# One block of TensorE matmuls for the spread of 1/den, and fixed order lists, in a four-layer attention and FFN kernel

## The chip, the cores and the metric

The kernel runs on one core of a Trainium2 chip. The metric is the device time of one execution in microseconds (us), the median of several runs; lower is better. The engines of the core are named as in the profile: PE (TensorE, matmuls), PEld (its weight loads), DVE (VectorE), ACT (ScalarE), POOL (GpSimd) and SP (the queue that issues most DMAs).

## The reference, cut to what matters

```python
x = A_x                                   # 2048 tokens x 512, bfloat16
x = x + _A_ref(_layernorm(x), A_wqkv, A_wo)
x = x + _B_ref(_layernorm(x), B_w_gate, B_w_up, B_w_down)
x = x + _A_ref(_layernorm(x), A_wqkv, A_wo)
x = x + _B_ref(_layernorm(x), B_w_gate, B_w_up, B_w_down)

# A: linear attention, 32 heads of 16
phi = lambda t: jnp.where(t > 0, t + 1, jnp.exp(t)) + 1e-6
pq, pk = phi(q), phi(k)
kv  = einsum("bhsd,bhse->bhde", pk, v);   z = einsum("bhsd->bhd", pk)
num = einsum("bhqd,bhde->bhqe", pq, kv);  den = einsum("bhqd,bhd->bhq", pq, z) + 1e-6
A = (num / den) @ wo
# B: (silu(x @ w_gate) * (x @ w_up)) @ w_down, inner width 1792
```

Layers 0 and 2 are A, layers 1 and 3 are B.

## The kernel before, in words

The 2048 tokens are 16 tiles of 128 tokens, in four groups of 512. Everything stays in SBUF; each weight is read once. TensorE's program is the string `PROGRAM`, one token for one block of matmuls; the first digit is the layer:

- `S` is a warm-up matmul on zeros. `0t3` transposes tile 3 on PE; all other transposes are DMAs issued from SP.
- `0k3` projects the keys of tile 3, `0q21` the queries of group 2, chunk 1. Four matmuls of 512 columns each.
- `0g3` adds tile 3 into X'·phi(k), a sum that holds four PSUM banks over all sixteen tiles; `0z3` adds its keys into z (four matmuls of one column), in one bank more. `0v` and `0m0` to `0m3` turn that sum into the matrix that is applied to the queries.
- `0d21` is the part of den of group 2, chunk 1. After its fourth part DVE takes 1/den.
- `0w5` applies the matrix to the scaled queries of tile 5 and adds the result to x. It starts the layer norm of the next layer for that tile.
- `1u309` is gate and up of group 3, inner block 9 (eight matmuls); `1n5` is down of tile 5 (fourteen).

1/den stands by token and has to be spread over the queries, which stand transposed. For most groups ACT repeats it (L713) and a DMA transposes it (L717). For the groups named in `PE_T` (`0d2` and `2d1`) the function `rep_pe` does it on PE: the tokens `0r2a`, a = 0 to 3, multiply 32 rows of `rT` with 32 rows of the selector `esel`, into one PSUM bank, four matmuls of 128 columns for each a. DVE then multiplies the queries with that bank (L742, called pqn below). The four blocks stand apart in `PROGRAM`: `0r21 0r23 0w3 0r22 0w2 0w1 0r20 0w0`, and `2r10 2v 2q33 2m1 2m0 2m2 2m3 2w0 2d31 2r11 2d30 2w1 2r13 2w2 2w3 2r12`.

Every instruction is an `Op` with the buffers it reads and writes. The queues of ACT, DVE, POOL and SP are ordered by a planner, `Prog.schedule`: it plays PE's fixed order with a cost for each operation (`occ`, `lat`), a wait of `SEM` between engines, and takes at each step the ready operation with the earliest due time, shifted by a `BIAS` for its kind. `ON_ACT` says where work has a choice: `0x5` puts the last step of a layer norm (called apply below: L509 on ACT, L513 on DVE) on ACT, `0s4` the statistics of a tile in layer 0 (L486 and L489 on ACT, L478 and L480 on DVE), `0k5` or `0q21` one of the steps of phi (L561), `0G0` and `0M0` copies out of PSUM. `sync` turns the buffers into semaphore waits. Each engine runs its own queue strictly in order.

A layer norm is: statistics, vpe (L498, POOL or DVE), pow (L502, POOL, 1/sqrt), nmr (L506, POOL, only for an apply on ACT), apply, and the DMA transpose (L522, SP) into `xnT`. `bank()` gives the PSUM bank that was used longest ago and is not pinned. The weights Wo, Wg and Wu are nine DMAs on POOL that wait for all transposes of layer 0 (`after=a`); POOL has four DMA lanes, so its fifth DMA waits in POOL's queue until the first has landed. `mask` is built on POOL by a memset and two selects (L414, L415, L418); `0z` ends with a multiplication by it, called zm (L641, DVE), before the first `0d`.

Of the kernel before, what the change touches and what calls it, by code (L numbers as in the profile page):

```python
# [5 lines left out]
ACT = mybir.ActivationFunctionType  # L6
# [3 lines left out]
P = 128  # L10

SEM = 0.06
HOLD = 0.17
BIAS = {"aggr": -2.4, "apply": 2.89, "den": 5.86, "evac": 3.27, "exp": -1.25, "gst": 0.77, "h": 5.8, "id1":
        -1.31, "mask": 3.19, "negm": -2.54, "phi": -6.05, "pow": 9.11, "pqn": -5.7, "rT": 3.11, "rep":
        -15.2, "res": -0.19, "sq": 1.71, "stats": -6.49, "tanh": -7.7, "ts": 1.82, "vpe": -3.12, "xT": 2.81,
        "zm": 2.36}


class Op:  # L20
    __slots__ = ("i", "eng", "fn", "deps", "occ", "lat", "dma", "lane", "start", "end", "need", "val",
                 "dead", "succ", "pos", "prio", "kind")


class Prog:
# [5 lines left out]
    def __init__(self, lanes):  # L31
        self.ops = []
        self.bufs = {}
        self.lanes = lanes

    def op(self, eng, fn, r=(), w=(), occ=0.5, lat=None, after=(), dma=0.0, prio=None, kind=""):
        o = Op()
        o.i = len(self.ops)
        o.eng, o.fn, o.occ, o.dma, o.prio, o.kind = eng, fn, occ, dma, prio, kind
        o.lat = lat if lat is not None else occ + 0.09  # L40
        o.need = dma > 0
        o.succ = []
        deps = set(a.i for a in after if a is not None)
        for k in r:
            st = self.bufs.get(k)
            assert st is not None and st[0] is not None, f"read of {k} before a write"
            deps.add(st[0])
        for k in w:
            st = self.bufs.get(k)
            if st:  # L50
                if st[0] is not None:
                    deps.add(st[0])
                deps.update(st[1])
        for k in r:
            self.bufs[k][1].append(o.i)
        for k in w:
            self.bufs[k] = [o.i, []]
        deps.discard(o.i)
        o.deps = deps
        self.ops.append(o)  # L60
        return o

    def schedule(self):
        ops = self.ops
        for o in ops:
            for d in o.deps:
                ops[d].succ.append(o.i)
        t = sum(o.occ for o in ops if o.eng == "pe")
        after = t
        for o in reversed(ops):  # L70
            dead = t + 50.0
            for s in o.succ:
                s = ops[s]
                dead = min(dead, s.dead - o.lat - SEM)
            if o.eng == "pe":
                dead = after = min(dead, after - o.occ)
            o.dead = dead if o.prio is None else o.prio
        for o in ops:
            o.dead -= BIAS.get(o.kind, 0.0)
        nd = {o.i: len(o.deps) for o in ops}  # L80
        free = {e: 0.6 for e in self.ENGINES}
        free["act"] = 0.61
        avail = {e: [] for e in self.ENGINES}
        pe_q = [o for o in ops if o.eng == "pe"]
        pe_at = 0
        order = {e: [] for e in self.ENGINES}
        pipe = [0.0, 0.0]

        def ready_time(o):
            rt = 0.0  # L90
            for d in o.deps:
                p = ops[d]
                if p.eng == o.eng and o.eng == "pe":
                    continue
                rt = max(rt, p.end + SEM)
            return rt

        rt_of = {}

        def push(o):  # L100
            rt_of[o.i] = ready_time(o)
            if o.eng != "pe":
                avail[o.eng].append(o)

        for o in ops:
            if nd[o.i] == 0:
                push(o)
        left = len(ops)
        while left:
            best = None  # L110
            for e in self.ENGINES:
                if e == "pe":
                    if pe_at < len(pe_q) and nd[pe_q[pe_at].i] == 0:
                        o = pe_q[pe_at]
                        s = max(free[e], rt_of[o.i])
                        if best is None or s < best[0]:
                            best = (s, o)
                    continue
                if not avail[e]:
                    continue  # L120
                at = {o.i: max(free[e], rt_of[o.i]) for o in avail[e]}
                lim = min(at.values()) + HOLD
                o = min((o for o in avail[e] if at[o.i] <= lim), key=lambda o: (o.dead, o.i))
                if best is None or at[o.i] < best[0]:
                    best = (at[o.i], o)
            assert best is not None, "stuck"
            s, o = best
            o.start = s
            free[o.eng] = s + o.occ
            if o.dma:  # L130
                k = o.lat > 2.5
                pipe[k] = max(pipe[k], s + o.occ + 0.9) + o.dma
                o.end = pipe[k] + 0.6
            else:
                o.end = s + o.lat
            if o.eng == "pe":
                pe_at += 1
            else:
                avail[o.eng].remove(o)
            o.pos = len(order[o.eng])  # L140
            order[o.eng].append(o)
            left -= 1
            for k in o.succ:
                nd[k] -= 1
                if nd[k] == 0:
                    push(ops[k])
        self.order = order
        self.span = max(o.end for o in ops)
        return order

    def sync(self):
# [3 lines left out]
        for e in self.ENGINES:  # L155
            for o in order[e]:
                if o.dma:
                    n = self.lanes[e]
                    k = rr.get(e, 0)
                    rr[e] = (k + 1) % n  # L160
                    o.lane = f"q{e}{k}"
# [32 lines left out]
        for e in self.ENGINES:  # L194
            seen = {}
            for o in order[e]:
                ws = []
                for q, p in o.deps.items():
# [3 lines left out]
                    ws.append((p.end, q, p.val))  # L202
                ws.sort()
                self.waits[o.i] = [(q, v) for _, q, v in ws]
# [51 lines left out]
S S S S S S S S S 0t0 S S S S 0t3 0t1 0k0 0t2 0k1 0k2 0g0 0k3 0z0 0g1 0k4 0g2 0g3 0k5 0z4 0k10 0z2 0k9 0g4 0g5  # L256
0k6 0z10 0k7 0z9 0z3 0q03 0k8 0g10 0t15 0g7 0k15 0k13 0z5 0z8 0k12 0g9 0k11 0q11 0g6 0z15 0k14 0q10 0z13 0q02
0z7 0z1 0q01 0g11 0q00 0z14 0q12 0q21 0z12 0z6 0z11 0q13 0d02 0d03 0d01 0d00 0g8 0d11 0q20 0g13 0d12 0q22 0d13
0d10 0q23 0d20 0g15 0g12 0g14 0d23 0d22 0d21 0q30 0v 0q31 0m0 0m1 0m3 0m2 0r21 0r23 0w3 0r22 0w2 0w1 0r20 0w0
0q33 0w5 0w11 0w7 0w6 0w9 0q32 0d33 0w8 0w4 0w10 1u011 1u007 1u005 1u008 0d31 1u002 1u006 0d32 1u012 1u003  # L260
1u013 0d30 1u010 1u004 1u000 1u110 1u001 1u009 0w14 1n3 0w12 1n0 1u106 1n1 1u102 1n2 1u107 1u204 0w13 1u101
0w15 1u111 2k2 1u109 1u105 1u103 1u104 1u108 2k0 2k1 1u100 2q00 1u112 1u113 2k3 1n7 1n6 1u209 1u211 1u205 1n4
1n5 1u213 1u200 1u303 1u202 1u203 2q10 1u301 1u208 1u309 1u304 1u206 1u212 2g0 1u201 1u311 1u302 2q11 1u305
1u207 1u310 2q01 1u308 2q03 1u312 2q02 1u210 1n11 1u313 2k4 1u300 1n8 1n10 1u306 1n9 1u307 2k8 1n14 2k7 2k10
2k5 2q21 1n15 2k6 2k9 1n13 2k11 1n12 2q12 2k15 2k14 2g3 2g5 2q20 2q22 2z4 2k13 2q23 2z15 2z9 2z7 2g2 2k12 2z3
2z14 2g7 2z6 2z8 2z2 2z11 2g6 2z5 2z12 2z13 2z0 2g14 2z1 2z10 2q13 2d01 2g12 2g1 2d02 2d00 2d03 2d20 2d13 2d21
2d22 2q30 2d10 2d12 2g13 2g10 2d11 2d23 2q31 2g15 2g4 2g9 2g11 2g8 2q32 2r10 2v 2q33 2m1 2m0 2m2 2m3 2w0 2d31
2r11 2d30 2w1 2r13 2w2 2w3 2r12 2w6 2w5 2w11 2w4 2w8 2w7 2d32 2w9 2w10 2d33 3u008 3u000 3u009 3u013 3u010
3u004 3u003 3u005 3u007 3u103 3u110 3u108 3u012 3u002 3u001 3u006 3u104 2w13 3u011 3n3 2w12 3u100 3n2 3n0
3u106 3u105 3u107 3u111 3n1 2w14 3u102 3u109 3u112 3u101 3u113 3n4 3n5 3n6 3n7 3u200 3u201 3u202 3u203 3u204  # L270
2w15 3u205 3u206 3u207 3u208 3u209 3u210 3u211 3u212 3u213 3n8 3n9 3n10 3n11 3u300 3u301 3u302 3u303 3u304
3u305 3u306 3u307 3u308 3u309 3u310 3u311 3u312 3u313 3n12 3n13 3n14 3n15
"""

PE_T = set("""
0t0 0t1 0t2 0t3 0d2 0t15 2d1
# [5 lines left out]
0G0 0G2 0G3 0M0 0M2 0k11 0k13 0k14 0k15 0k3 0k4 0k5 0k6 0p0 0p14 0p15 0p2 0q00 0q01 0q03 0q11 0q12 0q22 0q30  # L282
0q31 0s4 0s8 0t0 0t12 0t13 0t14 0t2 0t3 0t4 0t5 0t6 0t7 0x1 0x10 0x11 0x12 0x15 0x5 0x6 0x7 0x8 1p11 1p5 1p6
1p8 1t0 1t10 1t13 1t14 1t3 1t8 1x1 1x10 1x11 1x12 1x14 1x2 1x4 1x5 1x6 1x8 1x9 2G0 2G2 2M0 2M2 2k0 2k1 2k10
# [627 lines left out]
```

## Time and profile before

| what | value |
|---|---|
| time, median of 4 runs | 432.83 us (432.17 to 433.08) |
| the profiled execution's own time | 432.01 us |
| its span | 430.3 us |
| PE busy | 420.9 us (98%), 2231 matmuls |
| DVE, ACT, POOL busy | 290.6, 215.0, 79.7 us |

The span is the profiled part of the execution; 1.7 us lie around it. "Busy" of PE counts pipelined matmuls, so that four matmuls of 512 columns follow each other every 0.86 us while a single one is listed with 379 ns. In a timeline row the columns are the start, the length, the engine, the line, the operation with output and inputs, and the count; in brackets the idle time before it and what ended it.

### The profile page before, as it was taken

What the parts mean: (1) busy time and instruction counts of PE and PEld (TensorE: products, weight loads), DVE (VectorE), ACT (ScalarE), POOL (GpSimd) and SP (SyncE); (2) the same over time, 40 slices, a digit from 0 to 9 for tenths busy, and PEclk for the clock granted to TensorE, in tenths of its full rate; (3) what the DMA queues carried; (4) which work ended last, traced back from release to release, by engine and by line L of the source; (5) the groups of instructions that cost most, each with busy time, mean ns of one, the idle gap of its engine ahead of it and who ended that gap; (6) DMA issues with size and microseconds to landing.
All of it is one profiled execution on the core that took longest, in us unless ns stands there. A gap on an engine that the chain in (4) does not pass through costs nothing.

```text
span 430.3 us, 6541 instructions
## 1 busy us (share of the span) xinstructions
PE 420.9 (98%) x2231; PEld 194.6 (45%) x2231; DVE 290.6 (68%) x593; ACT 215.0 (50%) x402; POOL 79.7 (19%) x231
## 2 busy tenths in 40 slices
PE   6999999999999999999999999999999999999997
PEld 2444544444444444444444454444444444444444
DVE  6966998695687448776454549989836727845762
ACT  5997785684445444254456737593422403412320
POOL 5842046213210220000213100631010100000000
PEclk9999999999999999999999999999999999999999
DMA  8659234642110020000111104242020210001001
GB/s 276 144 86 356 57 75 128 118 84 41 37 37 2 12 26 12 2 0 2 26 24 27 24 14 87 50 91 45 12 50 13 26 37 14 12 17 34 1 2 50
DMA packets 52738, 23.11 MB, mean 54 GB/s; under 512 B 45856, under 2 KB 51616, under 8 KB 52704
## 3 DMA queue, kind: packets, MB, share of 16 engines
q1 hardware_dynamic: 50864, 16.13, 17.9%
q0 software_dynamic: 1296, 6.03, 4.1%
q10 hardware_dynamic: 544, 0.52, 0.4%
q8 instruction: 18, 0.29, 0.3%
q14 instruction: 16, 0.13, 0.1%
HBM read 9.70 MB, written 2.10 MB: 27 GB/s over the span
## 4 chain that ended last, share of the span: by engine, by line
PE 88%; ACT 3%; DMA 2%; POOL 2%; DVE 2%; issue 1%; SPq 0%; ACTq 0%; DVEq 0%
PE pb L395 88%; DMA xnT<-xnB 2%; POOL rstd L502 1%; ACT xnA L509 1%; DMA X<-in_A_x_dram 1%; ACT xnB L509 1%; ACT etmp L558 1%; DVE stats L478 0%; POOL nmr L506 0%; POOL vpe L498 0%; DVE tht L775 0%; ACT pk L561 0%; ACT tht L773 0%; SPq L522 0%; ACT xnB L489 0%
## 5 line engine op out<-in xcount | busy, mean ns | idle before, releaser
L773 ACT ACTIVATE tht<-pb 128x512 f32<-128x512 f32 x112 | 66.2, 594 | 116.0 <-PE pb L395 113.7
L395 PE MATMUL pb<-xnT,Wg 128*128 128x512 bf16 x448 | 114.9, 379 | 0.7 <-DMA xnT<-xnB 0.7
L395 PE MATMUL pb<-xnT,Wu 128*128 128x512 bf16 x448 | 114.9, 379 | 0.4 <-DVE tht L775 0.4
L775 DVE SCALAR_TENSOR_TENSOR tht<-tht,pb 128x512 f32<-128x512 f32 x112 | 76.8, 685 | 34.8 <-ACT tht L773 30.6
L395 PE MATMUL pb<-Wd,hT 128*128 128x512 bf16 (+1 forms) x462 | 99.8, 373 | 0.0
L778 DVE TENSOR_TENSOR hT<-tht,pb 128x512 bf16<-128x512 f32 x112 | 77.0, 688 | 11.6
L395 PEld LDWEIGHTS pb<-Wd,hT 128*128 128x128 bf16 x462 | 45.2, 98 | 51.7 <-DVE hT L778 0.4
L395 PEld LDWEIGHTS pb<-xnT,Wu 128*128 128x128 bf16 x448 | 43.7, 98 | 53.7 <-ACT xnB L489 0.7
L395 PEld LDWEIGHTS pb<-xnT,Wg 128*128 128x128 bf16 x448 | 43.4, 98 | 52.8 <-issue 1.3
L492 POOL TENSOR_SCALAR mv<-sums 128x1 f32<-128x1 f32 x50 | 11.9, 241 | 200.7 <-DVE X L753 113.0
L558 ACT ACTIVATE etmp<-pb 128x512 bf16<-128x512 f32 x64 | 37.2, 596 | 14.7 <-PE pb L395 12.2
L502 POOL TENSOR_TENSOR rstd<-vpe,negh 128x1 f32<-128x1 f32 x64 | 36.5, 571 | 32.1 <-DVE vpe L498 28.1
L563 DVE TENSOR_SCALAR etmp<-etmp 128x512 bf16<-128x512 bf16 x64 | 18.7, 292 | 23.1 <-ACT etmp L558 22.5
L801 DVE SCALAR_TENSOR_TENSOR pq<-pb,X 128x512 bf16<-128x512 f32 (+1 forms) x17 | 11.2, 660 | 32.6 <-PE pb L395 32.6
L395 PE MATMUL pb<-Wqkv,xnT 128*128 128x512 bf16 x128 | 31.7, 379 | 0.8 <-ACT xnT L544 0.4
L395 PE MATMUL pb<-xnT,Wqkv 128*128 128x512 bf16 x128 | 32.4, 378 | 0.0
L395 PE MATMUL pb<-GT,pq 128*128 128x512 bf16 x128 | 30.6, 379 | 1.3 <-DVE pq L742 0.9
L395 PE MATMUL pb<-pk,xnA 128*128 128x512 bf16 x128 | 31.0, 378 | 0.0
L489 ACT ACTIVATE xnB<-X,sums 128x512 bf16<-128x512 bf16 x32 | 22.9, 715 | 13.9 <-DVE X L753 6.2
L801 DVE SCALAR_TENSOR_TENSOR X<-pb,X 128x512 bf16<-128x512 f32 x16 | 11.1, 692 | 18.8 <-PE pb L395 18.7
L509 ACT ACTIVATE xnA<-X,nmr,rstd 128x512 bf16<-128x512 bf16 x23 | 18.6, 812 | 10.2 <-POOL nmr L506 10.0
L753 DVE SCALAR_TENSOR_TENSOR X<-pb,X 128x512 bf16<-128x512 f32 x32 | 21.6, 686 | 0.8 <-PE pb L395 0.7
(70 smaller groups left out, 306.5 us busy)
## 6 DMA issues: line engine op xcount, KB each, us to landing
out_dram<-pq SPq DMA_DIRECT2D x15, 128.0 KB, 1.7
Wg<-in_B_w_gate_dram POOLq DMA_DIRECT2D x4, 448.0 KB, 5.3
Wu<-in_B_w_up_dram POOLq DMA_DIRECT2D x4, 448.0 KB, 5.2
X<-in_A_x_dram SPq DMA_DIRECT2D x6, 256.0 KB, 4.8
Wd<-in_B_w_down_dram POOLq DMA_DIRECT2D x3, 512.0 KB, 4.8
Wqkv<-in_A_wqkv_dram SPq DMA_DIRECT2D x2, 512.0 KB, 7.1
Wqkv<-in_A_wqkv_dram ACTq DMA_DIRECT2D x2, 256.0 KB, 3.5
X<-in_A_x_dram SPq DMA_DIRECT2D x4, 128.0 KB, 3.5
```

What stands on the lines that cost most here:

```text
L395: return op("pe", lambda e: e.matmul(o_ap, lhsT=lhsT, rhs=rhs, start=start, stop=stop, skip_group_check=skip), r=r, w=w, occ=occ, lat=occ ...
L489: op("act", lambda a: a.activation(out=b_ap, in_=X[:, t, :], func=ACT.Square, scale=-float(D), bias=sums[:, t:t + 1], accum_out=mv[:, t, 1 ...
L492: op("pool", lambda p: p.tensor_scalar(out=mv[:, t, 0:1], in0=sums[:, t:t + 1], scalar1=-1.0 / D, scalar2=None, op0=ALU.mult), r=[f"sm{t}" ...
L502: op("pool", lambda p: p.tensor_tensor(out=rstd[:, t:t + 1], in0=vpe[:, t:t + 1], in1=negh[:], op=ALU.pow), r=[f"vp{t}", "negh"], w=[f"rs{ ...
L509: op("act", lambda a: a.activation(out=b_ap, in_=X[:, t, :], func=ACT.Identity, bias=nmr[:, t:t + 1], scale=rstd[:, t:t + 1]), r=[xk, f"nm ...
L558: op("act", lambda a: a.activation(out=etmp[e][:], in_=PB[pb][:], func=ACT.Exp), r=[f"pb{pb}"], w=[f"e{e}"], occ=0.48, lat=0.55, kind="exp")
L563: op("dve", lambda v: v.tensor_scalar(out=etmp[e][:], in0=etmp[e][:], scalar1=1.0, scalar2=1e-6, op0=ALU.min, op1=ALU.add), r=[f"e{e}"], w ...
L753: op("dve", lambda v: v.scalar_tensor_tensor(out=X[:, t, :], in0=PB[pb][:], scalar=1.0, in1=X[:, t, :], op0=ALU.mult, op1=ALU.add, accum_o ...
L773: op("act", lambda e: e.activation(out=tht[a][:], in_=PB[pg][:], func=ACT.Tanh, scale=0.5), r=[f"pb{pg}"], w=[f"th{a}"], occ=0.48, lat=0.5 ...
L775: op("dve", lambda v: v.scalar_tensor_tensor(out=tht[a][:], in0=tht[a][:], scalar=1.0, in1=PB[pg][:], op0=ALU.add, op1=ALU.mult), r=[f"pb{ ...
L778: op("dve", lambda v: v.tensor_tensor(out=hT[h][:, j, :], in0=tht[a][:], in1=PB[pu][:], op=ALU.mult), r=[f"pb{pu}", f"th{a}"], w=[f"h{h}_{ ...
L801: op("dve", lambda v, pb=pb, lo=lo, hi=hi: v.scalar_tensor_tensor(out=o_ap[:, lo:hi], in0=PB[pb][:, 0:hi - lo], scalar=0.5, in1=X[:, t, lo ...
```

## The change

1. `rep_pe` is one block for each group: token `0r2` (and `2r1`) takes four banks at once and issues its sixteen matmuls chunk by chunk, the four 32-row groups in turn, each into its own bank. Four pqn follow on DVE, one for each bank. In `PROGRAM` it stands as `0m3 0r2 0w3 0w2 0w1 0q33 0w0` and `2g8 2r1 2q32 2v 2q33 2m0 2m1 2m2 2m3 2d31 2d30 2w0 2w1 2w2 2d32 2w3`.
2. The planner with its costs goes. Each operation has a name, and `ORDER` gives the queue of ACT, DVE, POOL and SP as a written list. `ON_ACT` is another set: in layer 0, seven tiles instead of two have their statistics on ACT (2, 7, 10, 11, 12, 13, 15), and one apply instead of nine is there.
3. On POOL, the second select of `mask` (`i.c7`) stands behind the nine weight loads (`i.ld` to `i.ld8`), which follow the last layer norm of layer 0 in one run.
4. Tile 15 is no longer transposed on PE (`0t15`), but by a twelfth DMA transpose on SP.
5. The warm-up is 60 matmuls of 128 columns between the first blocks, in a pinned bank, instead of 13 of 512.
6. The last tile's down projection is cut into 384 and 128 columns instead of 256 and 256.

New functions `z_add` and `z_sum` are there, but no token uses them.

```diff
-        def rep_pe(L, g, a):
-
-            pb = bank()
+        def rep_pe(L, g):
             d = db[L, g][1]
             r_den.done(d)
-            ps = slice(a * H, (a + 1) * H)
+            bs = [bank(pin=True) for _ in range(P // H)]
             for c in range(NC):
-                mm(pb, esel[ps, c * HC:(c + 1) * HC, :].rearrange("p h j -> p (h j)"), rT[d][ps, :], True, True,
-                   r=[f"rT{d}", f"esel{a}"], w=[f"pb{pb}"], occ=MM128, cols=(c * P, (c + 1) * P), skip=True)
+                for a, pb in enumerate(bs):
+                    ps = slice(a * H, (a + 1) * H)
+                    mm(pb, esel[ps, c * HC:(c + 1) * HC, :].rearrange("p h j -> p (h j)"), rT[d][ps, :], True, True,
+                       r=[f"rT{d}", f"esel{a}"], w=[f"pb{pb}"], n=P, cols=(c * P, (c + 1) * P), skip=True)
...
+            for a, pb in enumerate(bs):
+                ap = pq[b][:].rearrange("p c (t a i) -> p c t a i", t=TG, a=P // H)[:, :, :, a]
+                by = PB[pb][:].rearrange("p (c t i) -> p c t i", c=NC, t=TG)
+                op("dve", lambda v, ap=ap, by=by: v.tensor_tensor(out=ap, in0=ap, in1=by, op=ALU.mult),
+                   r=ks + [f"pb{pb}"], w=ks, kind="pqn")
+                pinned.discard(pb)
...
     def schedule(self):
...
+        self.order = {"pe": [o for o in self.ops if o.eng == "pe"]}
+        for e in self.ENGINES[1:]:
+            by = {o.name: o for o in self.ops if o.eng == e}
+            self.order[e] = [by.pop(x) for x in ORDER[e].split()]
...
+ORDER = {
...
+    "pool": """
...
+0x15.pow 0x12.vpe 0x8.pow 0x12.pow 0x12.negm 0x13.negm 0x11.negm 0x11.pow 0x13.vpe 0x11.nmr 0x13.pow 0x14.pow i.ld
+i.ld1 i.ld2 i.ld3 i.ld4 i.ld5 i.ld6 i.ld7 i.ld8 i.c7 1x3.negm 1x3.vpe 1x3.pow 1x2.negm 1x2.vpe 1x2.pow 1x1.negm
...
 PE_T = set("""
-0t0 0t1 0t2 0t3 0d2 0t15 2d1
+0d2 0t0 0t1 0t2 0t3 2d1
...
-            for lo, hi in ((0, D // 2), (D // 2, D)) if last else ((0, D),):
+            for lo, hi in ((0, 3 * P), (3 * P, D)) if last else ((0, D),):
...
+        warm = bank(pin=True)
+
         def spin():
-            warm = bank()
-            mm(warm, zero[:, 0:P], zero, True, True, r=[f"h1_{NF - 1}"], w=[f"pb{warm}"], occ=0.427)
+            mm(warm, zero[:, 0:P], zero[:, 0:P], True, True, r=[f"h1_{NF - 1}"], w=[f"pb{warm}"], n=P, cols=(0, P))
```

## The prediction

> **What bounds the kernel now.** I read the page's busy row first, then PE's waits, then PE's timeline wherever it has a gap, last the engines that end those gaps.
>
> ```profile
> PE 420.9 (98%) x2231; PEld 194.6 (45%) x2231; DVE 290.6 (68%) x593; ACT 215.0 (50%) x402; POOL 79.7 (19%) x231
> ...
> PE 88%; ACT 3%; DMA 2%; POOL 2%; DVE 2%; issue 1%; SPq 0%; ACTq 0%; DVEq 0%
> ```
>
> PE is the bound: a full busy row and 88% of the chain that ended last. So only three things can change the time: PE's own work, PE's gaps, and the two ends. The matmuls stay the same apart from details, hence I look for the gaps.
>
> ```profile
> PE pb L395 <- DVE pq L742: 0.9, 1, 0.9
> PE pb L395 <- DMA xnT<-xnB: 0.7, 1, 0.7
> PE pb L395 <- DVE tht L775: 0.4, 2, 0.2
> ```
>
> After the first 26 us PE waits only some 2.3 us in all. The 0.9 stands behind a pqn of layer 2, which the change touches. The early stage and the blocks of `rep_pe` read like this:
>
> ```profile
> 11.47 1.04 PE L395 MATMUL pb<-Wqkv,xnT 128*128 128x512 bf16 x4 [0.41 <-ACT xnT L544]
> ...
> 55.15 0.41 PE L395 MATMUL pb<-rT,esel 32*128 32x128 bf16 x8
> 55.53 1.03 PE L395 MATMUL pb<-GT,pq 128*128 128x512 bf16 x4
> 56.50 0.39 PE L395 MATMUL pb<-rT,esel 32*128 32x128 bf16 x4
> 56.83 1.90 PE L395 MATMUL pb<-GT,pq 128*128 128x512 bf16 x8
> ...
> 266.08 1.02 PE L395 MATMUL pb<-GT,pq 128*128 128x512 bf16 x4 [0.41 <-ACT GT L649]
> ...
> 271.91 1.25 PE L395 MATMUL pb<-GT,pq 128*128 128x512 bf16 x5 [0.85 <-DVE pq L742]
> ```
>
> At 11.47 only two key blocks are done: the head costs about 9 us of PE, and is a chain of layer norms. A lone block of four small matmuls takes 0.32 to the next start, and stands 0.10 behind the block before it (55.53 + 0.86 = 56.39, but it starts at 56.50). Eight in a row take 0.38: the second four, on other rows, cost only 0.06.
>
> ```profile
> 12.00:26.00 14.00, 13.64 (x86) 6.29 (x85) 12.06 (x36) 13.63 (x25) 9.95 (x27) 1.00 0.59 105
> ...
> 29.19 0.97 POOL L428 DMA_DIRECT2D Wo<-in_A_wo_dram  x1 [4.73 <-DMA xnT<-xnA]
> ...
> 39.24 0.54 POOL L428 DMA_DIRECT2D Wu<-in_B_w_up_dram  x1 [0.59 <-DMA Wg<-in_B_w_gate_dram]
> ...
> 42.52 0.21 DVE L641 TENSOR_TENSOR Zm<-pb,mask 128x32 bf16<-128x32 f32 x1
> ```
>
> From 12 to 26 us (columns PE, PEld, DVE, ACT, POOL) ACT is as full as PE, 13.63 of 14. POOL is blocked by weight DMAs from the last transpose until 39.8, and zm runs at 42.52. Both matter below.
>
> **The change part by part.**
>
> *Layer 0, up to the first den block (43.20 before).* I walked the new lists with this trace's durations, taking starts of neighbours on one engine where they overlap: on DVE 0.60 for statistics, 0.32 for an apply, 0.62 for a read of PSUM; on ACT 1.46 for both statistics passes, 0.50 for an exp, 0.58 for a phi step, 0.72 for an apply; 2.45 from the issue of a DMA transpose to its landing, 1.2 to 1.3 per issue on SP. Tile 0's transpose starts 0.13 later (its apply now stands behind an aggregate), but its copy moves from ACT to DVE and `0k0` starts at 6.9 instead of 8.94, because tile 3 no longer comes first. `0k1` starts at 9.15 and `0k2` at 10.1 (11.47 before). Then PE waits for DVE and ACT: 0.9 for the second phi, 0.35 for `0g3`. At 26.8 PE has done what it had done at 27.9 before. The removed `0t15` is 0.22 more (four starts of 56 ns), paid for by one more SP issue of 1.2, behind which the transposes of tiles 8, 12, 13, 11 and 14 queue. So PE could be 1.2 earlier at the den block.
>
> The price is on POOL. The last transpose is issued at 27.7 instead of 26.08, so the weights start 1.6 later, at 30.8. In the trace the nine take 10.6 (29.19 to 39.78) because five wait for lanes; the run ends at 41.4, and only then comes the last mask select (0.41 in its row). zm, which needs it, ends at 42.1, and the den block cannot start before 42.2; everything on DVE behind zm waits as well. The gain is thus capped at 43.20 - 42.2 = 1.0.
>
> ACT is the doubt: five more statistics (5 x 1.46), eight applies less (8 x 0.72) and one phi step more (0.58) are +2.1 on a nearly full queue. I take -0.8; bounds -1.6 (transposes earlier) and +3.3 (rival 1). The new warm-up is 36 small matmuls ahead of tile 0 in the same 3.8 us; the granted clock is 1.00 in every window now, and I cost it at nothing, hidden behind the layer-norm wait.
>
> *The block in layer 0.* Before: 0.48 + 0.44 + 0.42 = 1.34 for the four quarters with their gaps. After: gap 0.10 + 0.32 + 3 x 0.06 = 0.60. The Trainium skill, "TensorE: Matmul & The Clock Gate", section "Measured speedup vs the span model", says that tiles of different rows run side by side and each adds some 4 ns; four rounds would then be 0.27 and the block 0.47. I keep the trace's 0.60; with no overlap at all it would be 16 x 0.056 + 0.2 = 1.1.
>
> A rule speaks against the change: "TensorEngine Tiling (Array Packing)", "Gotcha 1: PSUM Pressure": tiles of different rows write different banks, so all four must be free at once. Here the fourth bank held `0q31`, whose exp is the last of a row on ACT (three copies of GT at 0.52, then two queries at 1.1 each) and ends 0.4 after the block wants it. The row of before shows no such wait. By the rule the block loses 0.35 of its 0.74; without it, nothing. I take the rule: -0.4, bounds -0.75 and +0.2. Behind the block, the sums of `0w` need banks freed by four pqn, which are done in turn with the `0w` additions (0.62 each); none comes late.
>
> *The block in layer 2.* Before, from the end of `2g8` (261.50) to the first gate block (279.03): 17.53. After: three blocks and twelve `2w` at 0.863, `2v` 0.89, four den parts at 0.10 and the block 0.60 make 14.86. New waits: 0.06 for KVT behind two pqn on DVE, 0.33 for a den part whose bank waits for the fourth pqn, 0.26 for the third copy of GT on ACT: 15.5. The wait of 0.85 is gone, as the pqn are long done when `2w6` comes. But then the next thing is late: tile 3's layer norm, whose addition ends about 9.75 behind `2g8`, square and apply 13.4, transpose landed 16.0. So layer 3 starts at 16.0, not 15.5: -1.5. Bounds: -2.0, and -0.6 if DVE, full there (22.67 of 25 us), serves the norms later.
>
> *Between.* Layer 1's wait of 0.65 for the transposes of group 1 goes: the last is now issued ninth instead of eleventh, more than 2 us ahead of need. Against it, ACT's and DVE's lists are new everywhere, and I have not walked all of them. Before, some 1.1 of waits stand in layer 1; I allow the same again, so +0.4 net, bounds -1.1 and +1.5.
>
> *The end.* The last DVE operation is 128 columns instead of 256. By the rows for 512 (0.69) and 256 (0.42) it takes 0.28, and its output is half as large: -0.2, bounds -0.3 and 0. The same number of columns passes PE.
>
> Sum: -0.8 - 0.4 - 1.5 + 0.4 - 0.2 = -2.5. The profiled execution took 432.01, so 429.5 in its terms; it was 0.82 below the median of 432.83, so 430.3 for the median.
>
> **The rivals.**
>
> 1. *ACT becomes the bound of layer 0 (slower).* Up to 43.2 us ACT is busy 34.87 with overlaps; its new list is 41.7 by full row lengths. If neighbours stop overlapping, because each waits for its own semaphore, the list that starts at 5.4 ends near 47, the den block at 46.5 instead of 43.2: +3.3. With the other parts (-1.7) that is +1.6, or 434.4. It decides once the den block comes later than 44.9. For it: three key blocks run behind statistics of later tiles in ACT's order, and only three banks turn round. Against it: in before's fullest window ACT's neighbours do overlap. Chance 0.18.
>
> 2. *Layer 2's gain is taken back (a transfer is what counts).* If the layer norm of tile 3 lands 1.2 later, PE waits for it in place of the 0.85 and the quarters; with layer 0's early gain halved, the sum is -0.9: 431.9. Chance 0.16.
>
> 3. *It doesn't do what it says.* The sixteen matmuls don't overlap, the four banks come late in both layers, and mask and ACT eat the head: the sum is within 0.8 of nothing, 432.7. Chance 0.10.
>
> **How the numbers follow.** My forecast has 0.56, centred on 430.3, with 428.6 to 431.8 for itself. Slower by over 0.2% (0.87 us, about what a measurement of this kernel can tell from no change) comes from rival 1 and a sliver of rival 3: 0.19. Within it: rival 3, and the near ends of rival 2 and of the forecast: 0.11. Faster: 0.70. The range goes from 428.4 to 433.4: it covers all cases except a tail below and the larger half of rival 1.
>
> **What would show it.** In the profile after: `0k2` near 10.1; the den block near 42.2, with zm waiting for POOL rather than PE; rows "rT,esel" with x16 and 0.5 to the next start, with a gap in front in layer 0 ended by ACT etmp; no wait on DVE pq L742's successor, and instead one for a transpose ahead of layer 3. I would be wrong if the den block comes after 43.2, if PE's waits between 54 and 280 exceed 3 us, or if the sixteen take 0.9.

## Result, and the profile after

The changed kernel takes 431.58 us (median of 37 runs, 429.94 to 433.02) where the kernel before takes 432.9 (56 runs): a ratio of 0.9967, interval 0.9959 to 0.9975. It is 1.3 us faster. Its profiled execution took 430.35 us with a span of 428.6, against 432.01 and 430.3 before. It was 1.23 below its own median, before's 0.9 below: the comparison of the two traces holds for those two executions, and the profiles of the experiments show how far single executions scatter.

The page's busy rows and the split of the chain, of after:

```profile
PE 421.2 (98%) x2275; PEld 196.6 (46%) x2275; DVE 279.9 (65%) x625; ACT 205.0 (48%) x404; POOL 70.1 (16%) x192
...
PE 87%; DMA 5%; DVE 3%; ACT 2%; issue 1%; SPq 1%; POOL 0%; ACTq 0%
```

PE is still the bound, with the same work. DVE and ACT are each busy some 10 us less. The chain has 5% of DMA where it had 2%. Three of PE's waits in after (us in total, times, longest):

```profile
PE pb L410 <- DVE pq L574: 0.9, 1, 0.9
PE pb L410 <- DMA xnT<-xnB: 0.6, 1, 0.6
...
PE pb L410 <- DVE pq L751: 0.3, 1, 0.3
```

Gone are tht L775 (layer 1) and the 0.9 on pqn L742 (layer 2). The transpose row has changed its place, from layer 1 to the start of layer 3. The first of these rows is new, and the prediction did not have it. PE's timeline of after at the places that count:

```profile
47.93 2.75 PE L410 MATMUL pb<-pk,xnA 128*128 128x512 bf16 x12
51.53 0.46 PE L410 MATMUL pb<-Zm,pq 128*128 128x8 bf16 x12 [0.85 <-DVE pq L574]
...
55.69 0.67 PE L410 MATMUL pb<-rT,esel 32*128 32x128 bf16 x16
56.29 1.04 PE L410 MATMUL pb<-GT,pq 128*128 128x512 bf16 x4
...
260.13 0.40 PE L410 MATMUL pb<-rT,esel 32*128 32x128 bf16 x16
260.46 1.04 PE L410 MATMUL pb<-xnT,Wqkv 128*128 128x512 bf16 x4
...
264.80 0.36 PE L410 MATMUL pb<-Zm,pq 128*128 128x8 bf16 x8 [0.28 <-DVE pq L751]
...
276.68 1.02 PE L410 MATMUL pb<-xnT,Wg 128*128 128x512 bf16 x4 [0.62 <-DMA xnT<-xnB]
```

The two blocks are there as rows of x16: 0.60 to the next start in layer 0, 0.33 in layer 2. The wait at 51.53 is listed with 0.85; by the starts it costs 1.0 (3.60 behind the twelve matmuls ahead, which took 2.58 in before). The mask on POOL, zm on DVE, and DVE's rows behind the new wait:

```profile
41.96 0.37 POOL L431 TENSOR_SCALAR_AFFINE_SELECT mask<-mask 128x128 bf16<-128x128 bf16 x1
...
42.43 0.21 DVE L615 TENSOR_TENSOR Zm<-pb,mask 128x32 bf16<-128x32 f32 x1 [0.99 <-POOL mask L431]
...
50.71 0.43 DVE L733 TENSOR_TENSOR pq<-pq,RT 128x512 bf16<-128x512 bf16 x1 [1.19 <-DMA RT<-rrep]
51.06 0.42 DVE L574 TENSOR_TENSOR pq<-pq,etmp 128x512 bf16<-128x512 bf16 x1
```

DVE runs its list in order. The product L733 stands 1.19 us for its DMA-transposed 1/den; behind it stands L574, which finishes the queries that PE's next den part reads. PE waits for the second, but what is late is the first's DMA.

The table cuts the span at the starts of PE's rows, for the two traces and for four kernels of the experiments (e5, e7, e10 and c3 are explained below), in us:

| stage | before | after | e5 | e7 | e10 | c3 |
|---|---|---|---|---|---|---|
| span's start to first den block | 43.20 | 42.69 | 42.72 | 42.85 | 42.97 | 42.27 |
| to the first small block of `rep_pe` | 11.95 | 13.00 | 11.94 | 12.98 | 12.95 | 13.12 |
| to the first gate block of layer 1 | 13.47 | 12.80 | 14.78 | 13.66 | 12.81 | 12.90 |
| to the first matmul behind `2g8` | 192.88 | 191.64 | 194.85 | 192.32 | 193.59 | 191.46 |
| to layer 3's first gate block | 17.53 | 16.55 | 18.08 | 19.68 | 16.52 | 16.57 |
| to the end of the last DVE instruction | 149.15 | 149.23 | 149.15 | 149.99 | 149.23 | 149.25 |
| to the end of the span | 2.12 | 2.69 | 2.08 | 2.72 | 2.73 | 2.63 |

Before to after, line by line: -0.51, +1.05, -0.67, -1.24, -0.98, +0.08, +0.57, together -1.70, the difference of the spans.

### The profile page after: what moved, and what is told of

The parts are those of the page before. It is cut to its first block, busy times and chain, and to the rows that moved or that the text cites. A ratio compares the mean times of both kernels' runs of the same rounds, so it can differ in the third digit from the quotient of the medians.

```text
span 428.6 us, 6424 instructions
## 1 busy us (share of the span) xinstructions
PE 421.2 (98%) x2275; PEld 196.6 (46%) x2275; DVE 279.9 (65%) x625; ACT 205.0 (48%) x404; POOL 70.1 (16%) x192
## 4 chain that ended last, share of the span: by engine, by line
PE 87%; DMA 5%; DVE 3%; ACT 2%; issue 1%; SPq 1%; POOL 0%; ACTq 0%
PE pb L410 87%; DMA RT<-rrep 2%; DMA xnT<-xnA 1%; DMA X<-in_A_x_dram 1%; ACT pq L568 1%; DVE X L763 1%; ACT rrep L720 1%; DMA xnT<-xnB 1%; DVE stats L489 1%; ACT etmp L565 0%; DVE pq L574 0%; DVE pq L751 0%; SPq L441 0%; SPq L724 0%; DVE xnB L523 0%
## 5 line engine op out<-in xcount | busy, mean ns | idle before, releaser
L783 ACT ACTIVATE tht<-pb 128x512 f32<-128x512 f32 x112 | 65.1, 595 | 122.9 <-PE pb L410 90.2
L785 DVE SCALAR_TENSOR_TENSOR tht<-tht,pb 128x512 f32<-128x512 f32 x112 | 75.3, 683 | 64.6 <-ACT tht L783 60.5
L410 PE MATMUL pb<-Wd,hT 128*128 128x512 bf16 (+2 forms) x462 | 100.0, 373 | 0.0
L788 DVE TENSOR_TENSOR hT<-tht,pb 128x512 bf16<-128x512 f32 x112 | 73.8, 682 | 2.4
L502 POOL TENSOR_SCALAR mv<-sums 128x1 f32<-128x1 f32 x55 | 12.9, 240 | 177.4 <-DVE X L763 90.6
L570 DVE TENSOR_SCALAR etmp<-etmp 128x512 bf16<-128x512 bf16 x64 | 17.7, 288 | 19.8 <-ACT etmp L565 19.4
L499 ACT ACTIVATE xnA<-X,sums 128x512 bf16<-128x512 bf16 x23 | 16.5, 717 | 28.5 <-DVE X L811 28.5
L568 ACT ACTIVATE pq<-pb,onep 128x512 bf16<-128x512 f32 x25 | 17.1, 688 | 7.3 <-PE pb L410 7.2
```

What stands on the lines that cost most here:

```text
L410: return op("pe", lambda e: e.matmul(o_ap, lhsT=lhsT, rhs=rhs, start=start, stop=stop, skip_group_check=skip), r=r, w=w, n=n)
L499: op("act", lambda a: a.activation(out=b_ap, in_=X[:, t, :], func=ACT.Square, scale=-float(D), bias=sums[:, t:t + 1], accum_out=mv[:, t, 1 ...
L502: op("pool", lambda p: p.tensor_scalar(out=mv[:, t, 0:1], in0=sums[:, t:t + 1], scalar1=-1.0 / D, scalar2=None, op0=ALU.mult), r=[f"sm{t}" ...
L568: op("act", lambda a: a.activation(out=dst, in_=PB[pb][:], func=ACT.Identity, bias=onep[:]), r=[f"pb{pb}", "onep"], w=dk, kind="id1")
L570: op("dve", lambda v: v.tensor_scalar(out=etmp[e][:], in0=etmp[e][:], scalar1=1.0, scalar2=1e-6, op0=ALU.min, op1=ALU.add), r=[f"e{e}"], w ...
L783: op("act", lambda e: e.activation(out=tht[a][:], in_=PB[pg][:], func=ACT.Tanh, scale=0.5), r=[f"pb{pg}"], w=[f"th{a}"], kind="tanh")
```

## The experiments

Twelve kernels in three groups, each timed in five rounds. Ratios are to the kernel before in the same group; its medians were 432.53, 432.21 and 432.67. The lines of lists in the diffs are cut at both ends to the tokens that move.

### The head: mask, and the order on DVE

`e1_mask_first`, with the mask's second select ahead of the weights on POOL:

```diff
-0x13.pow 0x14.pow i.ld
-i.ld1 i.ld2 i.ld3 i.ld4 i.ld5 i.ld6 i.ld7 i.ld8 i.c7
+0x13.pow i.c7 0x14.pow i.ld
+i.ld1 i.ld2 i.ld3 i.ld4 i.ld5 i.ld6 i.ld7 i.ld8
```

> One change to the changed kernel: the second select of mask stands ahead of the last pow of layer 0 on POOL, no longer behind the nine weight loads. Theory A (the late mask holds zm, and with it the first den block and DVE's queue): zm no longer waits for POOL, the first den block starts 0.2 us earlier (42.46 instead of 42.69), the reciprocal and the first transposes of 1/den come 0.3 to 0.8 us earlier, and part of the 0.85 us wait of PE at 51.5 goes: 0.3 to 0.8 us faster than the changed kernel, ratio to the kernel before near 0.995. Theory B (DVE and ACT have slack there, and the transposes of 1/den are held by the weights' transfers): the first den block comes 0.2 earlier, the wait grows by as much, no change, ratio 0.9967.

431.08 us, 0.9969 (0.9957 to 0.9981). In its profile the den block comes at 42.29 and zm no longer waits for POOL, but PE's next wait reads:

```profile
51.35 0.46 PE L410 MATMUL pb<-Zm,pq 128*128 128x8 bf16 x12 [0.95 <-DVE pq L574]
```

Against after's profile the head is 0.40 earlier, the wait for DVE 0.10 longer, and the block of layer 0 only 0.18 earlier (55.51). Over half of the gain went into what follows, and the time is after's.

`e2_q23_first`, with the product that PE needs ahead of the one that waits:

```diff
-0q23.ts 0d0.pqn2 0q23.phi 0G1.evac
+0q23.ts 0q23.phi 0d0.pqn2 0G1.evac
```

> One change to the changed kernel: in DVE's list the last phi of group 2's queries stands ahead of the first product with a DMA-transposed 1/den (0d0.pqn2), which waits for its transfer. Theory A (DVE's fixed list holds a ready phi behind a transfer, and PE's den part waits for that phi): PE's wait of 0.85 us at 51.5 goes, 0.6 to 0.9 us faster than the changed kernel, ratio near 0.995. Rival (the wait is that of the transfer itself, and it shows up a few blocks later, at 0v or at the first 0w): within 0.2 us of the changed kernel, ratio 0.9967.

431.03 us, 0.9972 (0.9961 to 0.9983). The wait at 51.5 is gone. In its place PE's timeline of e2 has three at `0v`, two blocks later:

```profile
52.54 0.29 PE L410 MATMUL pb<-GT,Wqkv 128*128 128x128 bf16 x2 [0.18 <-ACT GT L658]
53.02 0.23 PE L410 MATMUL pb<-GT,Wqkv 128*128 128x128 bf16 x1 [0.20 <-ACT GT L658]
53.51 0.90 PE L410 MATMUL pb<-GT,Wqkv 128*128 128x128 bf16 x13 [0.26 <-ACT GT L658]
```

0.64 of 0.85 returns at ACT's copies of GT, and from den block to small block it takes 12.96 against 13.00. One wait had covered another.

### The block alone, the lists alone

`e3_row_groups_in_turn` keeps the block and the four banks, but issues the four matmuls of one 32-row group, then those of the next:

```diff
-            for c in range(NC):
-                for a, pb in enumerate(bs):
+            for a, pb in enumerate(bs):
+                for c in range(NC):
```

> One change to the changed kernel: the sixteen matmuls of a block are issued row group by row group (four chunks of one group, then the next) instead of in turn. Theory A (matmuls of different rows overlap only when they stand next to each other): the block in layer 2 takes 0.50 us to the next start (0.32 + 3 x 0.06, by the eight in a row of the kernel before) instead of 0.33, twice, so +0.2 to +0.3 us. Rival (the four banks alone bring the overlap, the turn does nothing): 0.33 again and the same time.

431.37 us, 0.9974 (0.9963 to 0.9985). The block takes 0.37 to the next start in layer 2, 0.04 more than interleaved, and 0.60 again in layer 0, where a wait sets its length (shown in the last part). Within the block the order hardly matters.

`e5_before_one_block` is before with the one block for each group, ordered by before's planner:

```diff
-... 0m3 0m2 0r21 0r23 0w3 0r22 0w2 0w1 0r20 0w0
+... 0m3 0m2 0r2 0w3 0w2 0w1 0w0
-2g8 2q32 2r10 2v 2q33 ... 2d31 2r11 2d30 2w1 2r13 2w2 2w3 2r12 2w6
+2g8 2r1 2q32 2v 2q33 ... 2d31 2d30 2w1 2w2 2w3 2w6
```

> The kernel before, its planner and costs kept, with the one edit that PE's list has `0r2` and `2r1` as one block of 16 matmuls over four banks where it had four blocks of four each; the DVE parts follow as the planner places them. Theory A (the block is worth the tilings it saves in both layers, and a little more in layer 2 where the last part comes earlier): layer 0 -0.6, the four blocks of layer 2 (measured .32 each with the gaps about .10 around each) -0.8, the wait of 0.85 for the quarter in layer 2 gone but 0.6 of it given back by the transposed tile: -1.2 to -1.7, ratio 0.996 to 0.9975, and layer 1 keeps before's waits (82.15, 84.25, 91.20; 1.5 us lost by the starts). Theory B (the gain of after is in the fixed lists, the block alone is hidden or lost by four banks pinned): ratio 0.999 to 1.001.

437.96 us, 1.0122 (1.0082 to 1.0163). Neither theory: the block, put into before's kernel, makes it slower. PE's timeline of e5 (its profiled execution was its fastest, 435.34):

```profile
55.97 0.39 PE L395 MATMUL pb<-rT,esel 32*128 32x128 bf16 x13 [1.08 <-ACT etmp L558]
...
69.44 1.02 PE L395 MATMUL pb<-xnT,Wg 128*128 128x512 bf16 x4 [0.47 <-DMA xnT<-xnB]
...
84.86 1.02 PE L395 MATMUL pb<-xnT,Wu 128*128 128x512 bf16 x4 [2.10 <-DVE tht L779]
...
282.37 1.02 PE L395 MATMUL pb<-xnT,Wg 128*128 128x512 bf16 x4 [1.64 <-DMA xnT<-xnB]
```

The first row is the price of four banks at once: of 16 matmuls, 3 run, and 13 wait 1.08 us for the exp that still reads the fourth bank. The others stand behind the block, where the planner has placed everything anew; which of its choices costs what no run separates.

`e6_planner_order` is the reverse: after's `PROGRAM`, `PE_T`, `ON_ACT`, block, 60 warm-ups and uneven last cut, put into before's kernel, so that its planner orders the other engines.

> The planner of before, with after's program: its PE list, its sets of tokens on PE and ACT, the block of 16 matmuls, the short spins and the uneven cut of the last output; only the order of DVE, ACT, POOL and of the transfers is the planner's and not a written list. Theory A (the lists bring the loss-free layer 1 of after, so its -1.3 to -1.5 goes back here): 432.3 to 432.8, ratio 0.9990 to 1.000, with waits of DVE tht, hT or of the transposes between 62 and 100 us. Theory B (after's PE list and its share of work on ACT bring it, whoever orders the other engines): 431.0 to 431.6, ratio 0.9965 to 0.998, no such waits.

445.78 us, 1.0295 (1.0268 to 1.0323): the direction of theory A, far beyond its number. One wait makes half of what it loses against after:

```profile
88.54 1.87 PE L395 MATMUL pb<-xnT,Wu 128*128 128x512 bf16 x4 [7.19 <-DVE tht L779]
```

The four matmuls behind it take 1.87 where others take 1.02: the granted clock is 0.81 from 88 to 100 us in this profile and 1.00 from 100 to 130. PE is busy 424.0 us for after's work (421.2), so the wait costs, by estimate, up to 2.8 us more than its own length.

`e7_quarters` is after with the four quarters in before's places in PE's list, and DVE's list to match:

```diff
-0m3 0r2 0w3 0w2 0w1 0q33 0w0
+0m3 0r21 0r23 0w3 0r22 0w2 0w1 0r20 0q33 0w0
-2g8 2r1 2q32 2v ... 2m3 2d31 2d30 2w0 2w1 2w2 2d32 2w3 2w6
+2g8 2q32 2r10 2v ... 2m3 2w0 2d31 2r11 2d30 2w1 2r13 2w2 2d32 2w3 2r12 2w6
```

> After with the one block undone: four blocks of four matmuls in the places that the PE list of before gives them, the DVE list adapted, all else after's. Theory A (the block is worth what before's rows show: layer 0 1.34 against 0.60, layer 2 four blocks of .42 against one of .42 and the 0.85 wait for the quarter back, less what the transpose in layer 2 takes): +1.0 to +2.0 against after, ratio to before 0.9990 to 1.001. Theory B (layer 3's start is held by the transpose of tile 3, so layer 2's quarters cost nothing; only layer 0's 0.6 shows): +0.4 to +0.8, ratio 0.9975 to 0.9985.

436.02 us, 1.0087 (1.0057 to 1.0116), over both theories. Layer 0 shows the price of quarters: 13.66 against 12.80, so 0.86, near the 0.74 that before's rows give for them (some 0.26 of it is a longer first `0w3`, 1.23 to the next start against before's 0.97). In layer 2 PE waits where it waited in before (0.41 and 0.85 there), but longer:

```profile
267.22 1.58 PE L410 MATMUL pb<-GT,pq 128*128 128x512 bf16 x4 [1.24 <-ACT GT L658]
...
274.47 2.76 PE L410 MATMUL pb<-GT,pq 128*128 128x512 bf16 x12 [1.60 <-DVE pq L748]
```

That makes 19.68 where before's own order of quarters takes 17.53. (Layer 3's 149.99 has a wait of 0.60 for a transpose in it.) So e7 measures the quarters in lists made for the block: block and lists fit each other. In the forms run here either alone is slower than before (1.0122, 1.0087); the two together are faster (0.9967).

`e11_block_twice` issues the block of layer 2 twice over:

```diff
-            for c in range(NC):
+            for c in [*range(NC)] * (1 + (L == 2)):
```

> After with the block of 16 in layer 2 alone issued twice over (the second pass writes the same values). It measures what the block costs by itself there, and whether layer 3's start is held by something that the block does not feed. Theory A (everything behind it, the transposed tile 3 too, hangs on the block's DVE parts and on PE's order): layer 3 starts 0.30 to 0.36 later against the end of `2g8`, ratio to before 0.9972 to 0.9980. Theory B (the 0.62 wait for the transposed tile swallows it): 16.6 as before, ratio 0.9963 to 0.9970.

431.3 us, 0.9954 (0.9932 to 0.9976), where after has 0.9967: no cost, but the interval leaves room for 1 us to either side, and the trace must decide (its profiled execution was its fastest, 429.36). PE's timeline of e11:

```profile
259.51 0.62 PE L410 MATMUL pb<-rT,esel 32*128 32x128 bf16 x32
260.07 1.04 PE L410 MATMUL pb<-xnT,Wqkv 128*128 128x512 bf16 x4
260.94 1.12 PE L410 MATMUL pb<-GT,Wqkv 128*128 128x128 bf16 x16
261.90 1.03 PE L410 MATMUL pb<-xnT,Wqkv 128*128 128x512 bf16 x4
...
275.84 1.04 PE L410 MATMUL pb<-xnT,Wg 128*128 128x512 bf16 x4 [0.42 <-DMA xnT<-xnB]
```

32 matmuls take 0.56 to the next start, 16 took 0.33: sixteen more cost 0.23 on PE. But `2v` (GT,Wqkv) then takes 0.96 to the next start, where after's takes 1.19 (261.34 to 262.53). In both, PE starts what follows `2v` 0.8 behind the end of ACT's second copy of GT. So the block is hidden behind those copies (e8 lists such a wait there, 0.18 for ACT's GT), a cover that neither theory had named: the 0.23 were gone before the wait for the transpose came. ACT comes to the copies late, having stood 1.9 us for a DMA transpose of 1/den in both. From the block's start to layer 3 it takes 16.33, against 16.55.

### Layer 1

`e8_d3_behind` moves one DVE token in layer 1:

```diff
-0d3.pqn2 1u009.gst 1u009.h 1u110.gst
+1u009.gst 1u009.h 0d3.pqn2 1u110.gst
```

> After with one token of the DVE list moved: the product of 1/den with pq of layer 0's last group that waits for a DMA-transposed 1/den in layer 1 (DVE at about 95 us) goes behind the next gate-and-up pair of h instead of ahead of it. In the profiles of the kernels with the mask moved, with the groups in turn and with the even cut PE waited 0.84 to 0.93 at 97.5 for that h, in the profile of after 0.5 on its weight load alone and nothing on the matmul. Theory A (that wait is there in most executions and after's profiled one was an exception): the wait is gone, -0.4 to -0.9 against after, ratio to before 0.9950 to 0.9960. Theory B (rarely there, or moved on to the product's own reader): within 0.2 of after, ratio 0.9965 to 0.9975.

431.05 us, 0.9965 (0.9948 to 0.9982): by the time it can't be told from after. The profiles say more (e8's own lost 0.36 in layer 2, at the copies of GT). This is what it takes away, as the timelines of e1 and, at the end, of after have it:

```profile
95.74 0.43 DVE L733 TENSOR_TENSOR pq<-pq,RT 128x512 bf16<-128x512 bf16 x1 [1.08 <-DMA RT<-rrep]
...
97.54 1.25 PE L410 MATMUL pb<-Wd,hT 128*128 128x512 bf16 x5 [0.93 <-DVE hT L788]
```

```profile
95.03 0.43 DVE L733 TENSOR_TENSOR pq<-pq,RT 128x512 bf16<-128x512 bf16 x1 [0.19 <-DMA RT<-rrep]
```

Again DVE stands for a transposed 1/den, with the h that PE needs behind it. Of the nine profiles that have this order there, six show the wait (0.81 to 1.08: e1, e3, e4, e7, e9, e10), and three don't (after, e2, e11), where DVE's wait for the transpose was short or none (0.19 in after). Two such transposes are on their way then, and the slower of them took 3.9 to 4.2 us from issue to landing in the six, 2.5 to 3.2 in the three. So the product waits for a transfer whose time varies from one execution to the next, and after's profiled execution was a lucky one; why the time varies is not known. The stretch from the first gate block to the first matmul behind `2g8` is 192.3 to 192.6 with the wait (e10, which has one more, apart), and 191.4 to 191.9 without. In e8 and c3, with the token moved, it is 191.45 and 191.46.

`e10_vpe_first` makes after's DVE list resemble before's in one place:

```diff
-1u006.gst 1u006.h 1x9.vpe
+1x9.vpe 1u006.gst 1u006.h
```

> After with one token of the DVE list moved: the small variance step (L508) of token tile 9 of layer 1 goes ahead of the gate-and-up pair that it follows, so that DVE stands still for ACT's sums of that tile (they end at 80.25) with that pair behind it, as DVE does in before at 80.76 ([2.19 <-ACT xnB]). Theory A (the in-order DVE behind that step is what cost before its waits for tht at 82.15 and 84.25, so the order of DVE brought layer 1's gain): PE waits again near 82 for the tht or hT of the pair, +0.4 to +0.9 against after, ratio 0.9975 to 0.9990. Theory B (slack enough on DVE; before's waits had another cause): within 0.2, ratio 0.9963 to 0.9973.

432.22 us, 0.9983 (0.997 to 0.9996), in theory A's range; in the same group e9, with after's layer 1, took 431.47 (0.9969, 0.9953 to 0.9985). The intervals overlap, so the profiles must decide. DVE's and PE's rows of e10, and then before's of the same layer:

```profile
80.52 0.15 DVE L508 TENSOR_SCALAR vpe<-mv 128x1 f32<-128x1 f32 x1 [2.03 <-ACT xnB L499]
...
81.01 1.03 PE L410 MATMUL pb<-xnT,Wg 128*128 128x512 bf16 x4
82.80 1.02 PE L410 MATMUL pb<-xnT,Wu 128*128 128x512 bf16 x4 [0.76 <-DVE tht L785]
```

```profile
80.76 0.15 DVE L498 TENSOR_SCALAR vpe<-mv 128x1 f32<-128x1 f32 x1 [2.19 <-ACT xnB L489]
...
82.15 1.02 PE L395 MATMUL pb<-xnT,Wu 128*128 128x512 bf16 x4 [0.22 <-DVE tht L775]
...
84.25 1.02 PE L395 MATMUL pb<-xnT,Wu 128*128 128x512 bf16 x4 [0.21 <-DVE tht L775]
...
91.20 1.02 PE L395 MATMUL pb<-xnT,Wg 128*128 128x512 bf16 x4 [0.65 <-DMA xnT<-xnB]
```

An operation of 0.15 us, put ahead of a gate-and-up pair, holds DVE for 2 us, and PE pays. The block at 82.80 starts 1.79 behind the one ahead instead of 0.86: 0.93 lost for a listed wait of 0.76. Over the stretch e9 takes 192.57 and e10 193.59. Before's two waits likewise cost 0.38 each by the starts of the rows (1.24 behind the block ahead instead of 0.86), and are listed with 0.22 and 0.21.

### The end

`e4_tail_halves` cuts the last tile evenly again:

```diff
-((0, 3 * P), (3 * P, D))
+((0, D // 2), (D // 2, D))
```

> One change to the changed kernel: the last tile's down projection is cut into 256 and 256 columns again. Theory A (the uneven cut lost time, since from the end of the last addition to the end of the span it is 2.7 us in the changed kernel and 2.1 in the one before): 0.3 to 0.6 us faster, ratio near 0.9957. Theory B (the smaller last piece gains its 0.14 us on DVE and the rest is chance of one execution): 0.1 to 0.2 us slower than the changed kernel, ratio 0.997.

432.0 us, 0.9982 (0.997 to 0.9993), no gain. From the last DVE instruction's end it takes 2.79, not before's 2.12: the uneven cut isn't what lengthens the end.

`e9_tail_in_turn` puts the last outputs in the order in which PE makes them:

```diff
-3n13.res 3n14.res 3n12.res 3n15.res 3n15.res1
+3n12.res 3n13.res 3n14.res 3n15.res 3n15.res1
-3n12.out 3n14.out 3n13.out 3n15.out 3n15.out1
+3n12.out 3n13.out 3n14.out 3n15.out 3n15.out1
```

> After with two places of its lists changed: DVE adds the residual of the last token tiles in the order 12, 13, 14, 15 in which PE makes them (after's list has 13, 14, 12), and SP sends the outputs in the same order (after's list has 12, 14, 13), so that they do not all leave behind tile 12's at 423.9. From the end of the last DVE instruction to the end of the span after takes 2.69 us, the same kernel with the even cut 2.8, before 2.12 and before with one block 2.1. Theory A (the bunched outputs are the 0.6): the stretch falls to 2.0 to 2.2, ratio to before 0.9945 to 0.9958. Theory B (the last transfer's own landing sets it): the stretch stays at 2.6 to 2.8, ratio 0.9963 to 0.9972.

431.47 us, 0.9969 (0.9953 to 0.9985). SP's rows of the outputs, after's first, then e9's:

```profile
423.93 2.39 SPq L441 DMA_DIRECT2D out_dram<-pq  x5
```

```profile
418.58 9.03 SPq L441 DMA_DIRECT2D out_dram<-pq  x5
```

The five outputs are spread over 9 us again, and the end still takes 2.69: theory B. What adds some 0.6 at the end stays open. It lies behind the last issue on SP, from whose end the span runs on for 2.28 us in after (426.32 to 428.6) and 1.71 in before (428.59 to 430.3). Everything with written lists shows it (2.63 to 2.79), before and e5 don't (2.12, 2.08), and e6 (the planner, but after's cut and after's count of 113 transfers on SP, against 112) lies between with 2.32.

### The moves together

`c3` is after with the moves of e1, e2, e8 and e9, and nothing else (their diffs above).

> After with four moves in its lists and nothing else: POOL makes the second half of the mask ahead of the run of weights, DVE has the exponential product of group 2's fourth tile ahead of the product that waits for a transposed 1/den, the layer-1 product of the last group stands behind a gate-and-up pair, and the last outputs go in turn. Theory A (the waits do not move on): -0.4 in the head, -0.6 at the second den part less 0.6 that returned at `0v`, -0.4 for layer 1 on average, -0.5 at the end: 430.0 to 430.6, ratio 0.9935 to 0.9955. Theory B (each wait moves to the next reader, only the end counts): ratio 0.9950 to 0.9962.

430.01 us, 0.9938 (0.9924 to 0.9952), at the edge of theory A's times, and faster than both kernels: its interval lies below after's (0.9959 to 0.9975). In its profile the den block comes at 42.27 and the wait in layer 1 is gone, while `0v` has the waits of e2 (0.23, 0.20 and 0.26) and the end takes 2.63. By the profiles its gain on the usual execution of after is thus the earlier den block (42.27; the nine profiles with after's order on POOL lie from 42.32 to 43.60, with a median of 42.98) and the wait in layer 1 that no longer comes.

## Why the prediction came out as it did

Forecast were 430.3 us, measured 431.58: by the medians a gain of 1.3, about half of the 2.5 forecast; between the two profiled executions it was 1.66. That the total came as close is luck. Layer 1, off by 1.6 to the good in one execution, pays for most of what was missing elsewhere (0.3, 1.05, 0.6 and 0.85). None of the three signs of being wrong came: the den block stood before 43.2, PE's waits behind 54 us were 0.9 in all, and the sixteen took 0.60.

- **Up to the first den block: -0.8 forecast, -0.51 between the two profiles, and no more than their scatter.** `0k2` came at 10.35 (forecast 10.1). The cap was right in kind: zm waits for POOL's mask (0.99 in its row), as the run of weights ended at 41.96 rather than 41.4, and the den block came at 42.69 rather than 42.2. But e5, which up to there issues what before issues, has its den block at 42.72, where before's profile has 43.20; and in the nine profiles with after's order on POOL the run of weights ends between 41.59 and 42.87, and the den block comes between 42.32 and 43.60. With the mask first it is 42.29 (e1) and 42.27 (c3). So that the new head gains anything by itself is not shown, nor what `ON_ACT`, tile 15's transpose and the warm-up each do to it.
- **Behind it: nothing forecast, +1.05 measured.** This is the step that was missing. The prediction walked layer 0 "up to the first den block" and then went on at the small block; between them DVE's new list has a product that waits for a transposed 1/den ahead of one that PE needs. Nearly all of the 1.05 is that wait (0.85 listed, 1.0 by the starts). It stands in every profile with after's order there; e1 shows that it swallows much of what an earlier mask gains, e2 that ACT's copies of GT stand behind it.
- **The block in layer 0: -0.4 forecast, -0.67 measured** up to the first gate block of layer 1. Nearly all of it is the block. Forecast were 0.10 + 0.50 + 0.35 of waiting for the fourth bank, 0.95 in all; measured were 0.11 + 0.60. Layer 2's row, without the wait, is 0.33, so the overlap is better than assumed and some 0.27 of the 0.60 is the wait. That it is the wait shows in the other profiles: ACT's exp ends 0.22 behind the block's start in after and 0.32 in c3 and e2, where the block takes 0.70; in e6 the exp is done 0.47 before, and the block takes 0.33. The Trainium skill's page "TensorEngine Tiling (Array Packing)", "Gotcha 1: PSUM Pressure", held: the four row groups write to four banks, and one bank that is still read stops the block, in e5 for 1.08 with three of the sixteen done. The other rule, from "TensorE: Matmul & The Clock Gate", section "Measured speedup vs the span model", was nearer than the 0.60 that I drew from the trace: by the estimate from that page the block would be 0.47 with its gap, and 0.42 was measured in layer 2 (0.33 and 0.09). Taking the 0.06 for the second four as the price of each further round was the error.
- **Layer 1: +0.4 forecast, -1.24 measured.** The mis-sized term. I let the wait of 0.65 for the transpose go, rightly, and allowed 1.1 of new waits, with before's other two left standing. In the profile hardly any came (PE is 0.21 late at 97.92, behind a weight load), and before's went: by their starts the three cost 0.38, 0.38 and 0.81 (91.20 is 1.67 behind the block ahead of it, instead of 0.86), 1.57 together. e10 shows in after's lists what brings such a wait as the first two, the place of a 0.15 us step on DVE; before with that step moved was not run. In six profiles of nine about 1 us is lost again near 98, and the stretch takes 192.3 to 192.6: against before's one profile (192.88) layer 1 then gains 0.3 to 0.6. That would be most of why after's median lies 1.23 above its profile; what puts before's median 0.9 above its own is not known.
- **Layer 2: -1.5 forecast, -0.89 measured** from the end of `2g8` (16.64 against 17.53). Here the next thing was named right: layer 3 waits 0.62 for tile 3's transpose, and the den part waits 0.28 for the fourth pqn (0.33 forecast). The transpose came late by more. DVE's apply of tile 3 ended at 13.9 behind `2g8` (13.4 forecast), the transpose landed at 16.39 (16.0), and PE started 0.24 after it. That the block is quicker than assumed brings nothing there, as e11 shows. The wait of 0.28 is also why the forecast that no wait on a pqn would be left, given among the signs, was wrong, though the sum had it.
- **The end: -0.2 forecast, +0.65 measured.** The last DVE operation took 0.29 as forecast (0.28), its output landed sooner (1.4 against 1.5), and still the last line of the table is 0.57 longer. The sum had no term for that, and its cause is open.
- **The rivals.** ACT did not become the bound of layer 0: the den block came well before 44.9. That layer 2's gain is taken back by a transfer happened in part, 0.64 of its 1.2. The rival that does least, "it doesn't do what it says", had the block wrong but the lists nearly right: in e1 and e2 the wait moved on.

## What to carry to other kernels

Where engines run fixed lists, an edit and the order around it belong together: the block under before's planner and after's lists with the quarters lost 5.8 and 3.8 us, and both together gained 1.3. Neither half had been tuned to stand alone. Look in each list for a cheap or patient operation that waits for a slow transfer or another engine with an urgent one behind it; the wait in the profile names the urgent one, and the row ahead of that one, on its engine, is the one that was held. Take several profiles before you trust a wait or its absence: the wait of 0.9 in layer 1 was in six profiles of nine, and not in the one that the first comparison used, and the start of the den block moved by 1.3 us between profiles with the same head.

## What the runs showed of the hardware

- Sixteen matmuls of 32 rows by 128 columns over four row groups and four banks took 0.33 us to the next start in layer 2, and sixteen more of the same 0.23, so 14 ns each; a lone block of four on one row group took 0.32 (before). Issued one group after the other, the sixteen took 0.37 (e3).
- The transposes of 1/den don't land at a steady time: DVE's wait for one at the same place was 0.19 in after and 1.08 in e1, where the slower of the two on their way took 3.2 and 4.1 us from issue to landing. Over the whole of after they took 2.4 to 4.1, with a median of 2.5.
- A listed wait is not the whole of what a stall costs PE: 0.76 was listed where the block came 0.93 late (e10), and 0.22 where it came 0.38 late (before).
- After a wait of PE of 7.19 us the granted clock was 0.81 from 88 to 100 us (e6).
